# Attention scores in three fp32r products instead of one fp32 product

## The chip, the cores and the metric

The kernel runs on one core of one Trainium2 chip. The metric is the time of one execution on the device in microseconds, as the median of several runs. Engines are named as in the profile: PE (TensorE, matmuls), PEld (TensorE, loads of the stationary operand), DVE (VectorE), ACT (ScalarE), POOL (GpSimd), SP (SyncE, which only issues DMAs here).

## The reference

Attention with a local window and global tokens over 8 batches and 8 heads, and behind it a two-layer network on all tokens (4352 tokens, 512 to 2048 to 512, softplus between). All of it in float32:

```python
k_all = np.concatenate([k_g, k_l], axis=2); v_all = np.concatenate([v_g, v_l], axis=2)
out_g = np.matmul(sm(scale * np.matmul(q_g, k_all.transpose(0, 1, 3, 2))), v_all)
mask = np.abs(pos[:, None] - pos[None, :]) <= 32
s_ll = np.where(mask, scale * np.matmul(q_l, k_l.transpose(0, 1, 3, 2)), -1000000000.0)
s_lg = scale * np.matmul(q_l, k_g.transpose(0, 1, 3, 2))
out_l = np.matmul(sm(np.concatenate([s_lg, s_ll], axis=-1)), v_all)
attn = np.concatenate([out_g, out_l], axis=2)          # 8 x 8 x (32 + 512) x 64
x = attn.transpose(0, 2, 1, 3).reshape(8 * 544, 512)
h = x @ w_in
out = (np.maximum(h, 0) + np.log1p(np.exp(-np.abs(h)))) @ w_out
```

## The kernel before

Two heads lie side by side on the 128 partitions (64 dimensions each), so there are 32 pairs of heads, m = 0 to 31, four to a batch. The first M0 = 6 pairs are done in a form of their own, at the start, while the weights arrive. The pairs m = 6 to 31 go through the functions `load`, `scores`, `maxima`, `probs`, `totals`, `values` and `normalise`. Each has three pieces p = 0, 1, 2, each with its own slice of queries and keys.

`scores(m, p)` computes the scores of one piece for both heads: two parts, each 128 keys (the stationary operand) against 192 queries (96 in the second part of p = 2). Head 0 uses partitions 0 to 63, head 1 partitions 64 to 127, and they write different PSUM banks. So one piece is 2 parts x 2 heads = 4 matmuls in fp32. DVE then adds the mask (L325) and takes maxima (L326). In the pairs m = 6 and 7 (`m < MPE`) the mask is added by a matmul instead.

The network is done batch by batch in 16 tiles of 128 hidden units. Its float32 operands are split into two halves in fp32r, a high half (`xh`, `gh`, slice 0 of `wi` and `wo`) and a low half (`xl`, `gl`, slice 1), and each product is made of three: high x high, high x low, low x high. For a tile, `hpart` makes h (24 matmuls of 512 columns in two calls), `act` makes the softplus (three steps on ACT, one on DVE), its high half gh on ACT (L547) and its low half gl on POOL (L548), and `opart` adds gh and gl times `wo` to four output tiles o (24 matmuls in two calls). `opart` comes one or two tiles behind. The weights are turned into float32 and split in `abs_w`, `bits_w` and `halves_w` (L481 to L499) while batch 0 runs. At the start of a batch `split_x` makes xh and xl from the attention's output (L453, L454).

Each `pieces()` entry has a due number, and `moe_items` counts the network's progress on the same scale (48 per batch, 12 per pair). The main loop issues network items and, whenever a due number is reached, the next attention piece. So a score piece stands between two runs of network matmuls on PE, about every 9 us, and a `values` piece once per pair. The code is recorded in this order, and a scheduler then sets the order on each engine by a simulated timeline. All matmuls are chained in the order written (`mm`), so it does not move them among themselves. It moves work on DVE, ACT and POOL.

Buffers that matter here: `raw` (queries and keys as loaded, three), and the tag `x`, whose two buffers hold the exponentials of the first six pairs and are free after that.

Of the kernel before, what the change touches and what calls it, by code (L numbers as in the profile page):

```python
# [8 lines left out]
F32 = mybir.dt.float32  # L9
F32R = mybir.dt.float32r  # L10
# [3 lines left out]
ALU = mybir.AluOpType  # L14
# [5 lines left out]
P = 128  # L20
# [4 lines left out]
QW = (288, 288, 192)  # L25
KWID = (256, 256, 256)
# [3 lines left out]

M0 = 6
MPE = 8
VAL = 22
TOT = 18
STEP = 3
# [14 lines left out]
def windows(ap2d, start, stride, count, width):  # L50
    base = ap2d[:, start:start + width]
    return bass.AP(base.tensor, base.offset, [list(base.ap[0]), [stride, count], [1, width]])
# [3 lines left out]
def moe_over_global_local_attention(  # L56
# [11 lines left out]
    nc = tc.nc  # L68
    PSUM = bass.MemoryType.PSUM
    const = ctx.enter_context(tc.tile_pool(name="const", bufs=1))  # L70
    pl = ctx.enter_context(tc.tile_pool(name="pl", bufs=2))
# [20 lines left out]
    for o, w, base, sign in ((32, 32, 0, 1), (64, 32, -96, -1), (96, 128, 32, 1), (96, 128, 32, -1)):  # L92
        r = mask0[:, 0, 1, o:o + w]
# [26 lines left out]
    def after(i, what):  # L120

        if what in order:
            tc.add_manual_dep(i.ins, order[what].name, mybir.DependencyInfo(mybir.DependencyClass.NoSync, mybir.DependencyReason.DATA), reason="order")
        return i

    def mm(*a, **k):
        order["pe"] = after(nc.tensor.matmul(*a, **k), "pe").ins  # L127


    M = B * H // 2  # L130
    st = {}
# [153 lines left out]
    def load(m, p):  # L285
        w = QW[p] + KWID[p]
        raw = pl.tile([P, 544], F32, tag="raw", name=f"raw{m}_{p}", bufs=3)
        order["load"] = nc.sync.dma_start(out=raw[:, :w], in_=qk[m - M0, :, EW[p]:EW[p] + w]).ins
        st["raw", m, p] = raw

    def load_v(m):
        t = pl.tile([P, 2, 6, D], F32, tag="v", name=f"v{m}", bufs=2)
        nc.sync.dma_start(out=t.rearrange("p h c d -> p (h c d)"), in_=v[m - M0])
        st["v", m] = t

    def scores(m, p):
        raw = st.pop(("raw", m, p))
        q = QW[p]
        if "o" not in banks:
            ps = ps_s.tile([P, 2, 512], F32, tag=("oA", "oB")[(3 * m + p) % 2], name=f"s_ps{m}_{p}")  # L300
        else:
            ps = ps_a.tile([P, 2, 512], F32, tag="a", name=f"s_ps{m}_{p}")
        parts = ((0, 0, 192), (192, 96, 192 if p < 2 else 96))
        pe_mask = m < MPE
        masks = (mask[:, 0:192], mask[:, 192:384] if p < 2 else mask5)
        for i, (o, qs, w) in enumerate(parts):
            ks = q + 128 * i
            for h in range(2):
                r = slice(64 * h, 64 * h + 64)
                mm(ps[:, h, o:o + w], lhsT=raw[r, ks:ks + P], rhs=raw[r, qs:qs + w],  # L310
                   start=True, stop=not pe_mask, skip_group_check=True)
            for h in range(2 if pe_mask else 0):
                mm(ps[:, h, o:o + w], lhsT=ident, rhs=masks[i], start=False, stop=True, skip_group_check=True)
        if p == 0:
            st["mt", m] = pl.tile([P, 348], F32, tag="mt", name=f"mt{m}", bufs=2)
            nc.gpsimd.memset(windows(st["mt", m], 0, 36, 3, 3), LOW)
        mt = st["mt", m]
        nb = 12 if p < 2 else 9
        s = pl.tile([P, 2, 32 * nb], F32, tag="s" if p < 2 else "s2", name=f"s{m}_{p}", bufs=4 if p < 2 else 2)
        if pe_mask:  # L320
            nc.scalar.copy(s, ps[:, :, 0:32 * nb])  # L321
        else:
            for o, mk in ((0, mask[:, 0:384]),) if p < 2 else ((0, mask[:, 0:192]), (192, mask5)):
                w = mk.shape[1]
                nc.vector.tensor_tensor(s[:, :, o:o + w], ps[:, :, o:o + w], mk.unsqueeze(1).to_broadcast([P, 2, w]), op=ALU.add)  # L325
        order["scores"] = nc.vector.tensor_reduce(windows(mt, 3 + 12 * p, 36, 2, nb), s.rearrange("p h (b k) -> p h b k", k=32),  # L326
                                axis=AX.X, op=ALU.max, apply_transpose=True).ins
        st["s", m, p] = s
# [20 lines left out]
    def maxima(m):  # L349
        e = fold(st.pop(("mt", m)), ALU.max)  # L350
        for a in range(1, 4):
            i = nc.vector.tensor_copy(e[32 * a:32 * a + 32, 0:42], e[0:32, 0:42]).ins  # L352
        order["maxima"] = i
        st["e", m] = e

    def probs(m, p):
        s, e = st["s", m, p], st["e", m]
        k = QW[p] // 32
        mb = pl.tile([P, 2, 288], F32, tag="mb", name=f"mb{m}_{p}", bufs=2)
        nc.vector.transpose(mb[:, :, :QW[p]].rearrange("p h (s k) -> p h s k", k=32),  # L360
                            windows(e, 7 * p, 21, 2, k).unsqueeze(3).to_broadcast([P, 2, k, 32]))
        for h in range(2):
            if p < 2:
                sw = s[:, h].rearrange("p (c w) -> p c w", w=192)
                nc.gpsimd.tensor_tensor(sw, sw, windows(mb[:, h], 0, 96, 2, 192), op=ALU.subtract)  # L365
        if p == 2:
            nc.gpsimd.tensor_tensor(s[:, :, 0:192], s[:, :, 0:192], mb[:, :, 0:192], op=ALU.subtract)
            nc.gpsimd.tensor_tensor(s[:, :, 192:288], s[:, :, 192:288], mb[:, :, 96:192], op=ALU.subtract)
        nc.scalar.activation(s, s, AF.Exp, scale=0.125)  # L369
        if p == 0:  # L370
            st["zt", m] = pl.tile([P, 348], F32, tag="zt", name=f"zt{m}", bufs=2)
            nc.gpsimd.memset(windows(st["zt", m], 0, 36, 3, 3), 0.0)
        nb = 12 if p < 2 else 9
        nc.vector.tensor_reduce(windows(st["zt", m], 3 + 12 * p, 36, 2, nb), s.rearrange("p h (b k) -> p h b k", k=32),  # L374
                                axis=AX.X, op=ALU.add, apply_transpose=True)

    def totals(m):
        e = fold(st.pop(("zt", m)), ALU.add)
        nc.vector.tensor_scalar(e[0:32, 0:42], e[0:32, 0:42], 1e-9, None, op0=ALU.add)
        nc.vector.reciprocal(e[0:32, 0:42], e[0:32, 0:42])  # L380
        for a in (2, 3, 1):
            o = 21 * (a // 2)
            nc.vector.tensor_copy(e[32 * a:32 * a + 32, 0:21], e[0:32, o:o + 21])
        rb = st["rb", m] = pl.tile([P, 640], F32, tag="rb", name=f"rb{m}", bufs=1)
        nc.vector.transpose(rb.rearrange("p (s k) -> p s k", k=32), e[:, 0:20].unsqueeze(2).to_broadcast([P, 20, 32]))

    def values(m):

        vt = st["v", m]
        ps = st["vs", m] = ps_a.tile([P, 2, 512], F32, tag="a", name=f"v_ps{m}")  # L390
        flat = ps.rearrange("p a q -> p (a q)")
        for p in range(NPC):
            s = st.pop(("s", m, p))
            for i, (o, qs, w) in enumerate(((0, 0, 192), (192, 96, 192 if p < 2 else 96))):
                c = OUT[p] + qs
                for h in range(2):
                    mm(flat[64 * h:64 * h + 64, c:c + w], lhsT=vt[:, h, 2 * p + i], rhs=s[:, h, o:o + w],
                       start=p < 2 and i == 0, stop=True, skip_group_check=True)
# [17 lines left out]
    def pieces():  # L416
        def piece(*fs):
            def go():
                for f in fs:
                    f()  # L420
            return go
        ps = []
        for m in range(M0, M):
            for p in range(NPC):
                fs = [lambda m=m, p=p: scores(m, p)]
                if m + 1 < M:
                    fs.append(lambda m=m, p=p: load(m + 1, p))
                if p == 2:
                    fs.append(lambda m=m: maxima(m))
                    fs += [lambda m=m, q=q: probs(m, q) for q in range(NPC)]  # L430
                ps.append((12 * m + 4 * p, piece(*fs)))
            ps.append((12 * m + TOT, lambda m=m: totals(m)))
            fs = [lambda m=m: values(m), lambda m=m: normalise(m)]
            if m + 2 < M:
                fs.append(lambda m=m: load_v(m + 2))
            ps.append((12 * m + VAL, piece(*fs)))
        ps.sort(key=lambda t: t[0])
        return ps
# [173 lines left out]
    def loads(upto):  # L612
        while wk[0] < min(upto, len(order_w)):
            if order_w[wk[0]]:
                load_w(*order_w[wk[0]])
            wk[0] += 1
# [12 lines left out]
    for p in range(NPC):  # L629
        load(M0, p)  # L630
    load_v(M0)
    load_v(M0 + 1)
    loads(W_PRE + 1)
    first = 12 * (H // 2 - 1) + VAL + STEP
    pcs = pieces()
# [5 lines left out]
    n = len(steps)  # L641
# [6 lines left out]
    for k in range(-2, n + 2):  # L648
# [9 lines left out]
        if held:  # L658
            r = bits_w(*held)
# [91 lines left out]
```

## Time and profile before

| | |
|---|---|
| median of 3 runs | 1004.74 us (1004.15 to 1005.12) |
| the profiled execution: its time | 1005.01 us |
| the profiled execution: its span | 1003.2 us |
| PE busy | 966.0 us, 96% |
| DVE, ACT, POOL busy | 645.8, 517.5, 446.1 us |
| first and last score matmul of a loaded piece | 73.5 and 822.3 us |
| mean granted PE clock | 0.987 |

The time of an execution holds its span and a little around it (1.8 us here). In a group's row stand the line, engine and operation, output and inputs with their sizes, the count, busy time in us, mean duration in ns, and the idle time of the engine just before with what ended it. Matmuls overlap in their pipeline, so their durations add up to more than the time they occupy; the chain of work shows the time that each adds. "x8" in a timeline is eight instructions that follow each other. All matmuls but the bf16 masks are shown as "f32", fp32r ones too.

### The profile page before, as it was taken

Reading aid. Unit: us, or ns where it says so; the run is one execution under the profiler, and the core shown is the slowest. Engines: PE = TensorE matmul, PEld = TensorE weight load, DVE = VectorE, ACT = ScalarE, POOL = GpSimd, SP = SyncE. Lnnn points to the kernel's source line nnn. Section 1 sums busy time; section 2 is a strip of 40 time slices with the busy share of each in tenths; the row PEclk is TensorE's granted clock in tenths of the full one; section 3 lists DMA queues with packets and bytes.
Section 4 is the critical chain, followed back from the end, with each engine's and each line's share of the span. In section 5 each row is a group of like instructions: output and inputs, shape, how many; then the busy total and the mean of one; then the engine's idle time right before and its main releaser. Section 6 shows DMA issues by size and latency. Waiting matters only on the chain.

```text
span 1003.2 us, 14264 instructions
## 1 busy us (share of the span) xinstructions
PE 966.0 (96%) x5151; PEld 755.1 (75%) x5151; DVE 645.8 (64%) x1348; ACT 517.5 (52%) x918; POOL 446.1 (44%) x603
## 2 busy tenths in 40 slices
PE   6798989899999999999999999999999999999996
PEld 4576767677777777777777777777777778888895
DVE  6885979856678766776667677776677665211210
ACT  5787656544445544454454444554445445444452
POOL 5664776524444444453345444444435344222221
PEclk9999989989999999999999999999999999999998
DMA  9824322211112111121112111211112100100000
GB/s 354 310 74 144 112 83 60 58 63 48 40 49 90 49 37 48 49 85 43 47 34 90 40 49 49 70 58 49 48 39 89 47 2 16 50 1 1 22 22 21
DMA packets 34302, 66.19 MB, mean 66 GB/s; under 512 B 7608, under 2 KB 11448, under 8 KB 34232
## 3 DMA queue, kind: packets, MB, share of 16 engines
q1 hardware_dynamic: 33416, 65.19, 20.4%
q8 instruction: 40, 0.66, 0.3%
q14 instruction: 30, 0.25, 0.1%
q10 hardware_dynamic: 816, 0.10, 0.1%
HBM read 55.84 MB, written 9.44 MB: 65 GB/s over the span
## 4 chain that ended last, share of the span: by engine, by line
PE 79%; DVE 1%; POOL 0%; issue 0%; ACT 0%; DVEq 0%; POOLq 0%
PE o L127 35%; PE h L127 34%; PE s_ps L127 5%; PE v_ps L127 5%; DVE xl L454 1%; DVE zt L374 0%; POOL wo L499 0%; DVE mb L360 0%; POOL gl L548 0%; DVE wbitswo L490 0%; DVE e L544 0%; ACT ot L566 0%; DVE wlastwo L493 0%; DVE mt L352 0%; DVE mt L342 0%
## 5 line engine op out<-in xcount | busy, mean ns | idle before, releaser
L127 PE MATMUL o<-wo,gh 128*128 128x512 f32 x1088 | 347.5, 400 | 6.2 <-ACT gh L547 4.9
L127 PE MATMUL h<-xh,wi 128*128 128x512 f32 (+1 forms) x1152 | 351.1, 388 | 1.2 <-DVE e L544 0.7
L548 POOL TENSOR_TENSOR gl<-e,gh 128x512 fp32r<-128x512 f32 x136 | 177.8, 1307 | 333.2 <-ACT gh L547 271.1
L127 PEld LDWEIGHTS h<-xh,wi 128*128 128x128 f32 x1152 | 210.3, 190 | 51.4 <-issue 5.6
L127 PEld LDWEIGHTS o<-wo,gh 128*128 128x128 f32 x1088 | 200.9, 189 | 58.3 <-ACT gh L547 5.8
L544 DVE SCALAR_TENSOR_TENSOR e<-h,e 128x512 f32<-128x512 f32 x136 | 93.0, 684 | 234.4 <-ACT e L543 213.9
L127 PE MATMUL h<-xl,wi 128*128 128x512 f32 (+1 forms) x576 | 220.5, 383 | 0.0
L127 PE MATMUL o<-wo,gl 128*128 128x512 f32 x544 | 216.2, 397 | 2.5 <-POOL gl L548 2.5
L541 ACT ACTIVATE e<-h 128x512 f32<-128x512 f32 x136 | 81.3, 598 | 232.2 <-PE h L127 232.2
L547 ACT CAST gh<-e 128x512 fp32r<-128x512 f32 x136 | 84.3, 620 | 112.6 <-DVE e L544 112.6
L365 POOL TENSOR_TENSOR s<-s,mb 128x384 f32<-128x384 f32 x104 | 107.0, 1060 | 51.1 <-DVE mb L360 51.1
L127 PEld LDWEIGHTS h<-xl,wi 128*128 128x128 f32 x576 | 109.0, 189 | 22.7
L127 PEld LDWEIGHTS o<-wo,gl 128*128 128x128 f32 x544 | 102.9, 189 | 27.1 <-POOL gl L548 3.3
L543 ACT ACTIVATE e<-e,one 128x512 f32<-128x512 f32 x136 | 98.4, 723 | 4.2
L542 ACT ACTIVATE e<-e 128x512 f32<-128x512 f32 x136 | 85.7, 630 | 3.4
L325 DVE TENSOR_TENSOR s<-s_ps,mask 128x768 f32<-128x768 f32 (+1 forms) x96 | 64.7, 695 | 29.4 <-PE s_ps L127 29.4
L369 ACT ACTIVATE s<-s 128x768 f32<-128x768 f32 (+1 forms) x78 | 61.7, 790 | 37.1 <-POOL s L365 34.7
L374 DVE TRANSPOSE_TENSOR_REDUCE zt<-s 128x24 f32<-128x768 f32 (+1 forms) x78 | 69.9, 902 | 6.3 <-ACT s L369 4.7
L326 DVE TRANSPOSE_TENSOR_REDUCE mt<-s 128x24 f32<-128x768 f32 (+1 forms) x78 | 69.3, 888 | 5.8 <-ACT s L321 5.1
L127 PEld LDWEIGHTS s_ps<-raw 64*128 64x128 f32 x624 | 48.7, 186 | 29.6 <-issue 22.1
L127 PE MATMUL s_ps<-raw 64*128 64x192 f32 (+1 forms) x624 | 70.1, 340 | 0.7 <-ACT e_g L174 0.7
L127 PEld LDWEIGHTS v_ps<-s,v 128*64 128x64 f32 x624 | 42.5, 137 | 14.3 <-issue 9.0
(134 smaller groups left out, 881.9 us busy)
## 6 DMA issues: line engine op xcount, KB each, us to landing
raw<-in_qk SPq DMA_DIRECT2D x52, 272.0 KB, 2.7
v<-in_v SPq DMA_DIRECT2D x26, 384.0 KB, 3.1
out<-ot SPq DMA_DIRECT2D x34, 256.0 KB, 2.1
wiraw<-in_w_in SPq DMA_DIRECT2D x16, 512.0 KB, 9.1
woraw<-in_w_out SPq DMA_DIRECT2D x16, 512.0 KB, 8.6
raw<-in_qk SPq DMA_DIRECT2D x26, 224.0 KB, 2.5
v<-in_v SPq DMA_DIRECT2D x6, 512.0 KB, 6.0
raw<-in_qk SPq DMA_DIRECT2D x6, 416.0 KB, 7.8
```

Of the source, the lines that this page charges most:

```text
L127: order["pe"] = after(nc.tensor.matmul(*a, **k), "pe").ins
L325: nc.vector.tensor_tensor(s[:, :, o:o + w], ps[:, :, o:o + w], mk.unsqueeze(1).to_broadcast([P, 2, w]), op=ALU.add)
L326: order["scores"] = nc.vector.tensor_reduce(windows(mt, 3 + 12 * p, 36, 2, nb), s.rearrange("p h (b k) -> p h b k", k=32), axis=AX.X, op=A ...
L365: nc.gpsimd.tensor_tensor(sw, sw, windows(mb[:, h], 0, 96, 2, 192), op=ALU.subtract)
L369: nc.scalar.activation(s, s, AF.Exp, scale=0.125)
L374: nc.vector.tensor_reduce(windows(st["zt", m], 3 + 12 * p, 36, 2, nb), s.rearrange("p h (b k) -> p h b k", k=32), axis=AX.X, op=ALU.add, a ...
L541: nc.scalar.activation(e, ph, AF.Abs)
L542: nc.scalar.activation(e, e, AF.Exp, scale=-1.0)
L543: nc.scalar.activation(e, e, AF.Ln, bias=one)
L544: nc.vector.scalar_tensor_tensor(e, ph, 0.0, e, op0=ALU.max, op1=ALU.add)
L547: nc.scalar.copy(gh, e)
L548: nc.gpsimd.tensor_tensor(gl, e, gh.bitcast(F32), op=ALU.subtract)
```

## The change

Pairs from m = 9 on (`SPLIT`) get their queries and keys split like the network's operands. A new function `split_qk` reads a loaded `raw` tile and writes a tile with two halves: the high one by a cast to fp32r on ACT, the low one by a subtraction on POOL. `scores` then makes each product as high x high + high x low + low x high, 12 matmuls to a piece instead of 4. The split of a piece is issued right behind the scores of the piece before it. Its tile takes the two buffers of the tag `x`. The pairs below 9 are unchanged.

```diff
+SPLIT = 9
...
+    def split_qk(m, p):
+
+        raw, w = st.pop(("raw", m, p)), QW[p] + KWID[p]
+        t = st["halves", m, p] = pl.tile([P, 2, 544], F32R, tag="x", name=f"qk{m}_{p}", bufs=2)
+        nc.scalar.copy(t[:, 0, :w], raw[:, :w])
+        nc.gpsimd.tensor_tensor(t[:, 1, :w], raw[:, :w], t[:, 0, :w].bitcast(F32), op=ALU.subtract)
...
     def scores(m, p):
-        raw = st.pop(("raw", m, p))
...
+        if m >= SPLIT:
+            t = st.pop(("halves", m, p))
+            products = ((t[:, 0], t[:, 0]), (t[:, 0], t[:, 1]), (t[:, 1], t[:, 0]))
+        else:
+            raw = st.pop(("raw", m, p))
+            products = ((raw, raw),)
         for i, (o, qs, w) in enumerate(parts):
             ks = q + 128 * i
-            for h in range(2):
-                r = slice(64 * h, 64 * h + 64)
-                mm(ps[:, h, o:o + w], lhsT=raw[r, ks:ks + P], rhs=raw[r, qs:qs + w],
-                   start=True, stop=not pe_mask, skip_group_check=True)
+            for n, (kt, qt) in enumerate(products):
+                for h in range(2):
+                    r = slice(64 * h, 64 * h + 64)
+                    mm(ps[:, h, o:o + w], lhsT=kt[r, ks:ks + P], rhs=qt[r, qs:qs + w],
+                       start=n == 0, stop=n == len(products) - 1 and not pe_mask, skip_group_check=True)
...
                 fs = [lambda m=m, p=p: scores(m, p)]
+                then = (m, p + 1) if p < 2 else (m + 1, 0)
+                if SPLIT <= then[0] < M:
+                    fs.append(lambda then=then: split_qk(*then))
                 if m + 1 < M:
                     fs.append(lambda m=m, p=p: load(m + 1, p))
```

How it stands on the engines, at two places. First PE in batch 1, at the piece p = 2 of pair 11. `o1_3` is an output tile of batch 1, `h1_11` the hidden tile 11 of batch 1, `s_ps11_2` the piece's scores; the numbers at the end count tiles. Before:

```order
L127 MATMUL o1_3_2163<-wo8_1319,gh1_8_2534 128x512 x2
L127 MATMUL o1_3_2163<-wo8_1319,gl1_8_2535 128x512
L127 MATMUL s_ps11_2_2643<-raw11_2_2414 128x192 x2
L127 MATMUL s_ps11_2_2643<-raw11_2_2414 128x96 x2
L127 MATMUL h1_11_2685<-xh1_0_2016,wi10_1230 128x512 x2
```

and now:

```order
L128 MATMUL o1_3_2188<-wo8_1319,gh1_8_2614 128x512 x2
L128 MATMUL o1_3_2188<-wo8_1319,gl1_8_2615 128x512
L128 MATMUL s_ps11_2_2734<-qk11_2_2668 128x192 x6
L128 MATMUL s_ps11_2_2734<-qk11_2_2668 128x96 x6
L128 MATMUL h1_11_2787<-xh1_0_2030,wi10_1230 128x512 x2
```

Nothing moved on PE; the piece alone has three times as many matmuls, and so at all 69 pieces.

Second POOL at the end of batch 0. `s8_*` are the exponentials' inputs of pair 8, `zt8` its sums, `wo15` the last tile of weights, `gl0_15` the low half of the last hidden tile of batch 0. Before:

```order
L367 TENSOR_TENSOR s8_2_1862<-s8_2_1862,mb8_2_1893 128x2x192
L368 TENSOR_TENSOR s8_2_1862<-s8_2_1862,mb8_2_1893 128x2x96
L316 MEMSET mt10_2278 128x3x3
L339 COPY zt8_1884<-zt8_1884 32x75 x3
L499 TENSOR_TENSOR wo15_1920<-wlastwo_1918,wo15_1920 128x512
L548 TENSOR_TENSOR gl0_15_1977<-e0_15_1971,gh0_15_1976 128x512
```

and now:

```order
L381 TENSOR_TENSOR s8_2_1862<-s8_2_1862,mb8_2_1896 128x2x192
L382 TENSOR_TENSOR s8_2_1862<-s8_2_1862,mb8_2_1896 128x2x96
L330 MEMSET mt10_2322 128x3x3
L353 COPY zt8_1887<-zt8_1887 32x75 x3
L297 TENSOR_TENSOR qk9_2_2112<-raw9_2_1869,qk9_2_2112 128x448
L516 TENSOR_TENSOR wo15_1923<-wlastwo_1921,wo15_1923 128x512
L565 TENSOR_TENSOR gl0_15_1980<-e0_15_1974,gh0_15_1979 128x512
```

The subtraction of pair 9's piece 2 now stands behind the copies of zt8 and ahead of wo15 and gl0_15. Its cast stands likewise just ahead of wo15's cast on ACT.

## The prediction

> **What bounds the kernel now.** I read the page first: how busy each engine is, and the chain of work that ended last.
>
> ```profile
> span 1003.2 us, 14264 instructions
> PE 966.0 (96%) x5151; PEld 755.1 (75%) x5151; DVE 645.8 (64%) x1348; ACT 517.5 (52%) x918; POOL 446.1 (44%) x603
> PE 79%; DVE 1%; POOL 0%; issue 0%; ACT 0%; DVEq 0%; POOLq 0%
> PE o L127 35%; PE h L127 34%; PE s_ps L127 5%; PE v_ps L127 5%; DVE xl L454 1%; DVE zt L374 0%; POOL wo L499 0%; DVE mb L360 0%; POOL gl L548 0%; DVE wbitswo L490 0%; DVE e L544 0%; ACT ot L566 0%; DVE wlastwo L493 0%; DVE mt L352 0%; DVE mt L342 0%
> ```
>
> TensorE carries the chain, and the scores (s_ps) are only 5% of it, about 50 us. So the ceiling of any gain is small, and each score piece pays its change in full wherever TensorE has no gap. The second view cuts the span into stretches; I asked for one batch of the middle (430 to 540 us) and for the turn from batch 0 to batch 1.
>
> ```profile
> 200.00:210.00 10.00, 8.61 (x23) 6.39 (x24) 4.99 (x14) 1.67 (x4) 2.45 (x3) 0.66 0.14 52
> 430.31:539.77 109.46, 109.46 (x577) 84.91 (x577) 79.22 (x175) 53.54 (x86) 49.65 (x72) 1.00 0.19 54
> ```
>
> The columns are TensorE, its weight loads, VectorE, ScalarE, GpSimd, granted clock, DMA share, GB/s. In the middle TensorE has no gap at clock 1.00. At 200 us it has one, at a granted clock of 0.66.
>
> **What a score piece costs before.** The chain in order of time shows two pieces between runs of 12 fp32r matmuls (start, length, what):
>
> ```profile
> 453.99 2.79 PE h L127 x12
> 456.78 0.85 PE s_ps L127 x8
> 457.63 2.96 PE o L127 x12
> ...
> 466.19 0.72 PE s_ps L127 x8
> ```
>
> The timeline of the weight loads shows what happens in the first of them:
>
> ```profile
> 456.71 0.63 PEld L127 LDWEIGHTS s_ps<-raw 64*128 64x128 f32 x8 [0.36 <-DVE zt L379]
> 456.72 0.29 PEld L127 LDWEIGHTS s_ps<-raw 64*128 64x128 f32 x3
> 456.98 0.19 PEld L127 LDWEIGHTS s_ps<-raw 64*128 64x128 f32 x2
> 457.14 0.19 PEld L127 LDWEIGHTS s_ps<-raw 64*128 64x128 f32 x2
> 457.56 0.30 PEld L127 LDWEIGHTS o<-wo,gh 128*128 128x128 f32 x2 [0.23 <-ACT e L541]
> ```
>
> A piece writes 4 matmuls and the trace shows 8: each fp32 matmul runs as two passes. The loads come two by two (one per head, on the two halves of the rows), so there are 4 slots of a pair. Loads 2 to 4 (456.72, 0.29 long) end at 457.01; a load lasts 0.19, so the second pair begins at 456.82, 0.11 after the first. The third begins at 456.98 and the fourth at 457.14, each 0.162 later, which is 192 columns at two cycles and 2.4 GHz (0.160) plus 0.002. So a slot is set by its columns, and the load of the next slot runs under it. From first load to the load of the following o: 0.108 (first load) + 3 x 0.162 + 0.160 (last stream) + r = 0.85, so r = 0.096 for changing over. The 0.72 of the piece p = 2, whose last two slots have 96 columns (0.080), is then 0.108 + 2 x 0.162 + L + 0.080 + 0.096, which leaves L = 0.112 for a slot whose columns would take only 0.082. That slot is set by its weight load. Three other rows, of the timeline and of the groups, bear on this load:
>
> ```profile
> 64.77 0.74 PEld L127 LDWEIGHTS o0g<-p0g1gh,v 128*128 128x128 f32 x6 [0.28 <-issue]
> L127 PEld LDWEIGHTS h<-xh,wi 128*128 128x128 f32 x1152 | 210.3, 190 | 51.4 <-issue 5.6
> L127 PEld LDWEIGHTS s_ps<-raw 64*128 64x128 f32 x624 | 48.7, 186 | 29.6 <-issue 22.1
> ```
>
> From the chain, for the rate of fp32r:
>
> ```profile
> 974.47 2.79 PE o L127 x12
> 982.88 2.82 PE h L127 x24
> ```
>
> Six loads of 128 columns with only 64 columns to stream between them take 0.74, so (0.74 - 0.19) / 5 = 0.11 each: the floor again. The fp32r loads of wi last 190 ns, the fp32 loads of the scores 186, so I expect the same floor for both. In fp32r, 512 columns take 2.79 / 12 = 0.233 and 256 take 2.82 / 24 = 0.1175: 0.45 ns a column plus 0.002, or 0.089 for 192 columns and 0.046 for 96.
>
> **The change, part by part.** 23 pairs of heads (m = 9 to 31) change, 46 pieces with p < 2 and 23 with p = 2. Each has 6 slots of one fp32r pass where it had 4 slots of one fp32 pass.
>
> *Score pieces.* Streaming falls from 4 x 0.162 to 6 x 0.089, but no slot can be shorter than its load. That price, s, is not in the trace for fp32r with 64 rows. Its low end is 0.112 (same weights, in fp32), its high end 0.1175 (fp32r, 256 columns, which the columns alone explain). Both are near; I take 0.115.
> - p < 2: 0.108 + 5 x 0.115 + 0.087 + 0.096 = 0.866, against 0.85: +0.016, times 46 = +0.7 us (ends: 0 and +1.3).
> - p = 2: 0.108 + 5 x 0.115 + 0.044 + 0.096 = 0.823, against 0.72: +0.103, times 23 = +2.4 us (ends +2.0 and +2.7).
> Sum +3.1 us (+2.0 to +4.0). The two edges (first load, r) may differ for fp32r by some 0.02 either way, 1.4 us over 69 pieces; I take 0 and keep it for the range.
>
> The Trainium skill (TensorE: Matmul & The Clock Gate, What overlaps and what doesn't) says that a weight load overlaps running matmuls only where the row group differs. The trace differs: the third pair of loads begins at 456.98, as the second pair of matmuls starts on the same rows, and 0.162 has no room for 0.108 + 0.160 in turn. If that rule held for fp32r alone, the sum would be that of the third rival below.
>
> *The split: 69 casts on ScalarE, 69 subtractions on GpSimd.* Priced by the same kind of work on 512 columns:
>
> ```profile
> L547 ACT CAST gh<-e 128x512 fp32r<-128x512 f32 x136 | 84.3, 620 | 112.6 <-DVE e L544 112.6
> L548 POOL TENSOR_TENSOR gl<-e,gh 128x512 fp32r<-128x512 f32 x136 | 177.8, 1307 | 333.2 <-ACT gh L547 271.1
> ```
>
> and the timeline around the last gl of batch 1:
>
> ```profile
> 310.29 1.29 POOL L548 TENSOR_TENSOR gl<-e,gh 128x512 fp32r<-128x512 f32 x1 [3.99 <-issue]
> 314.74 0.39 PE L127 MATMUL o<-wo,gl 128*128 128x512 f32 x1
> ```
>
> A cast of 544 columns is 0.66 us, a subtraction 1.39 (448 columns: 0.54 and 1.14). A batch adds 8 and 4 of them: 7.4 us to ScalarE's 53.5 and 15.7 to GpSimd's 49.6, of 109.5. The halves are made a whole piece (some 9 us, 456.78 to 466.19) before they are read. What waits behind a subtraction on GpSimd is gl, which TensorE reads. The last gl of batch 1 ends at 311.58 and is first read at 314.74, a cover of 3.2 us against one subtraction of 1.39. So I cost it at nothing in batches 1 to 7; without cover it would be up to 1.39 a piece. The q/k load now waits for the subtraction in place of the scores, and comes earlier: nothing, at a DMA share of 0.19.
>
> *The turn from batch 0 to 1.* Here there is no cover. The rows of GpSimd, ScalarE and TensorE:
>
> ```profile
> 198.53 1.18 POOL L339 COPY zt<-zt 32x75 f32<-32x75 f32 x3 [3.04 <-DVE zt L374]
> 199.82 1.29 POOL L499 TENSOR_TENSOR wo<-wlastwo,wo 128x512 fp32r<-128x512 f32 x1
> 201.06 1.28 POOL L548 TENSOR_TENSOR gl<-e,gh 128x512 fp32r<-128x512 f32 x1
> 199.07 0.62 ACT L498 CAST wo<-wlastwo 128x512 fp32r<-128x512 f32 x1 [2.30 <-DVE wlastwo L493]
> 202.40 0.80 PE L127 MATMUL o<-wo,gl 128*128 128x512 f32 x1 [0.73 <-POOL gl L548]
> 202.99 1.05 PE L127 MATMUL o<-wo,gh 128*128 128x512 f32 x2
> 208.97 0.62 PE L127 MATMUL o<-wo,gh 128*128 128x512 f32 x2
> ```
>
> The subtraction of qk9_2 is put on GpSimd's queue between the copies of zt and wo, so wo and gl come 1.14 later and so does TensorE, which reads that gl at once (201.06 + 1.28 = 202.34). (The cast stands ahead of wo's on ScalarE, where 2.30 us are idle: nothing.) From 202.40 to about 208.5 a pair of matmuls takes 1.05 instead of 0.62, at half the clock. If full speed returns at the same moment, 1.14 fewer microseconds are spent at half speed and half of the delay is won back: +0.6 us (ends 0 and +1.14).
>
> **Sum.** +3.1 + 0.6 = +3.7 us. The profiled execution took 1005.01 us around its span of 1003.2, 0.27 above the median of 1004.74, so on the median the forecast is 1008.4 us. The difference is 0.4%; about 0.2% (2.0 us) is what a measurement here can tell from no change.
>
> **Rivals.**
> 1. *Streaming decides, faster.* If the fp32r load of 64 rows took less than 0.089, each slot would be 0.089: p < 2 is 0.736 (-0.114), p = 2 is 0.607 (-0.113), 69 pieces -7.8, with the turn -7.2: 997.5 us. Its point is a load step of 0.104: there the pieces give back what the turn costs. For it: fp32 needs two passes where fp32r needs one. Against it: L = 0.112 for these very weights, and loads of 186 and 190 ns. The Trainium skill (FP8 and Floating Point Precision, TensorE Precision Notes) counts four passes for true fp32, so three products would be three quarters of the work; 0.160 for half a matmul of 192 columns agrees with four, but the rule counts no loads.
> 2. *fp32r is slower below 256 columns.* No fp32r matmul of the trace is narrower, so the 0.45 ns a column is not shown at 192. At the fp32 pass's two cycles a slot is 0.162: p < 2 is 1.17 (+0.32), p = 2 is 0.99 (+0.27), sum +21, with the turn about 1027. At four cycles a slot is 0.322 (p < 2 +1.28, p = 2 +0.93): +81, about 1086. For it: only the missing row. Against it: 256 and 512 columns lie on one line.
> 3. *Loads or heads in turn.* If a load could not run under the stream of its own rows, a slot is 0.112 + 0.089: p < 2 +0.45, p = 2 +0.45, sum +31, 1036 us. If the two heads did not run side by side, 12 slots of 0.112 give +0.67 and +0.76, sum +48, 1054. Against both: fp32 does neither here.
>
> **How the numbers follow.** Forecast (slots at the load step) 0.80; rival 1: 0.05; rival 2: 0.10; rival 3: 0.05. Range: the forecast's own bounds, 1004.74 + 2.0 + 0 - 1.4 = 1005.3 and 1004.74 + 4.0 + 1.1 + 1.4 = 1011.2, opened to 1005 and 1012 for small waits in batch 0, where GpSimd also gets two subtractions. What it leaves out is the 0.20 of the rivals. Faster: rival 1, 0.05. The same: the part of the forecast up to 1006.75 (low step, no delay at the turn), 0.17. Slower: the rest, 0.63 + 0.10 + 0.05 = 0.78.
>
> **What would show it.** In the profile after, a score piece should be 12 matmuls in 0.85 to 0.88 for p < 2 and 0.81 to 0.84 for p = 2, its loads in pairs 0.112 to 0.118 apart; TensorE still without a gap from 210 to 850 us; gl and wo about 1.1 us later near 201. It is wrong if pairs lie 0.09 apart (rival 1), 0.16 or more (rival 2), if loads come singly (rival 3), or if TensorE waits for gl or qk in the middle.

## The result, and the profile after

The changed kernel takes 1009.96 us (median of 4 runs, 1009.79 to 1011.17) against 1004.44 us (4 runs, 1003.79 to 1005.12) for the kernel before, measured beside it: ratio 1.0057, 95% interval 1.004 to 1.0075. That is 5.5 us slower. The forecast was 1008.4 us, 3.7 us slower.

The head of the page after the change, the same lines as the prediction shows of before: span, busy time of each engine, and the chain by engine.

```profile
span 1007.7 us, 15027 instructions
PE 968.8 (96%) x5427; PEld 763.0 (76%) x5427; DVE 660.5 (66%) x1348; ACT 553.0 (55%) x987; POOL 534.5 (53%) x672
PE 79%; POOL 1%; issue 1%; ACT 0%; POOLq 0%
```

PE is busy 2.8 us more (968.8 against 966.0), and the span is 4.5 us longer, so part of the loss is idle time on PE. POOL has 88.4 us more to do. The stretches show where PE idles (PE, PEld, DVE, ACT, POOL, granted clock, DMA share, GB/s):

```profile
150.00:175.00 25.00, 24.23 (x120) 18.48 (x116) 23.79 (x39) 14.03 (x24) 18.17 (x18) 1.00 0.30 81
200.00:210.00 10.00, 5.88 (x13) 3.98 (x14) 8.00 (x18) 1.80 (x3) 4.79 (x7) 0.66 0.18 60
210.00:850.00 640.00, 640.00 (x3620) 503.71 (x3619) 463.63 (x994) 346.01 (x565) 371.55 (x478) 1.00 0.18 50
```

From 210 to 850 us PE has no gap, as forecast. At the turn to batch 1 it is busy 5.88 of 10 us, before 8.61. The first row is a place that the prediction did not look at: late in batch 0, where DVE is busy 23.79 of 25 us. Before the change PE had no gap there:

```profile
150.00:175.00 25.00, 25.00 (x120) 19.70 (x117) 23.13 (x40) 15.89 (x27) 17.32 (x18) 1.00 0.21 61
```

The chain of the changed kernel in order of time, in batch 3, shows the score pieces (p < 2, then p = 2):

```profile
456.91 2.79 PE h L128 x12
459.71 0.84 PE s_ps L128 x12
460.55 2.96 PE o L128 x12
...
469.10 0.80 PE s_ps L128 x12
```

and the timeline of the weight loads shows the first of them:

```profile
459.64 0.74 PEld L128 LDWEIGHTS s_ps<-qk 64*128 64x128 f32 x12 [0.36 <-issue]
```

Twelve loads, two by two, take 0.74. A load lasts 0.19, so the pairs lie (0.74 - 0.19) / 5 = 0.11 apart. The piece p < 2 went from 0.85 to 0.84, the piece p = 2 from 0.72 to 0.80.

By stage, the traces compare like this. Each time is that of the first matmul of h with xl in that batch or hidden tile (us; the two middle columns are experiments 1 and 2, told below):

| | before | no pair 9 | pair 9 with one subtraction | after |
|---|---|---|---|---|
| batch 0, hidden tile 0 | 87.16 | 87.48 | 87.47 | 87.54 |
| batch 0, hidden tile 15 | 185.8 | 186.1 | 186.2 | 188.2 |
| batch 1 | 205.12 | 205.50 | 206.53 | 208.44 |
| batch 2 | 316.14 | 316.79 | 317.17 | 318.67 |
| batch 6 | 754.01 | 755.93 | 756.32 | 757.81 |
| end | 1003.2 | 1005.7 | 1005.8 | 1007.7 |

Batches 2 to 5 take 109.47 us each before and 109.79 after: +0.32, which is 4 pieces p = 2 at +0.08. (The 0.01 that each of the eight pieces p < 2 is shorter does not show in a batch.) Most of the rest arises ahead of batch 1: +2.4 by tile 15, of which 0.4 is there at tile 0 already, ahead of the first split, then +0.9 at the turn, and 0.8 less in batch 1, some of it won back at half clock. A last 0.5 lies behind the last matmul, where both kernels do the same work.

Where the +2.4 comes from shows in the timelines of the stretch at 163 us. VectorE before, and after:

```profile
163.40 0.41 DVE L488 TENSOR_SCALAR wbitswo<-wbitswo 128x512 int32<-128x512 int32 x1
163.73 0.67 DVE L544 SCALAR_TENSOR_TENSOR e<-h,e 128x512 f32<-128x512 f32 x1
164.33 0.15 DVE L346 COPY zt<-zt 32x6 f32<-32x6 f32 x1
164.40 0.67 DVE L490 SCALAR_TENSOR_TENSOR wbitswo<-woraw,wbitswo 128x512 int32<-128x512 int32 x1
165.01 1.28 DVE L379 TENSOR_SCALAR zt<-zt 32x42 f32<-32x42 f32 x1
...
168.37 1.52 DVE L383 COPY zt<-zt 32x21 f32<-32x21 f32 x3
...
171.87 0.68 DVE L544 SCALAR_TENSOR_TENSOR e<-h,e 128x512 f32<-128x512 f32 x1
```

```profile
163.97 1.60 DVE L505 TENSOR_SCALAR wbitswo<-wbitswo 128x512 int32<-128x512 int32 x1
165.50 1.26 DVE L360 COPY zt<-zt 32x6 f32<-32x6 f32 x1
166.68 0.67 DVE L561 SCALAR_TENSOR_TENSOR e<-h,e 128x512 f32<-128x512 f32 x1
...
167.88 0.17 DVE L393 TENSOR_SCALAR zt<-zt 32x42 f32<-32x42 f32 x1
...
170.13 2.70 DVE L397 COPY zt<-zt 32x21 f32<-32x21 f32 x3
...
174.80 0.68 DVE L561 SCALAR_TENSOR_TENSOR e<-h,e 128x512 f32<-128x512 f32 x1
```

POOL after, in the same stretch, with the two subtractions that the change puts into batch 0 (qk9_0 and qk9_1):

```profile
162.96 2.33 POOL L297 TENSOR_TENSOR qk<-raw,qk 128x544 fp32r<-128x544 f32 x1
165.24 1.49 POOL L516 TENSOR_TENSOR wo<-woraw,wo 128x512 fp32r<-128x512 f32 x1
...
169.78 1.57 POOL L297 TENSOR_TENSOR qk<-raw,qk 128x544 fp32r<-128x544 f32 x1
171.29 1.32 POOL L516 TENSOR_TENSOR wo<-woraw,wo 128x512 fp32r<-128x512 f32 x1
```

VectorE's shift of weight bits (L505, a TENSOR_SCALAR) grows from 0.41 to 1.60, a copy of zt (L360) from 0.15 to 1.26, and three copies (L397) from 1.52 to 2.70. The first two end close to the end of the POOL subtraction beside them: the shift at 165.57 (that of qk9_0 ends at 165.29), the copy at 166.76 (that of wo ends at 166.73). The copy of 32 x 6 elements also stands ahead of e now. Between 163.4 and 171.9 VectorE does the same work in both kernels, and the delay of the second e follows from the rows: 0.57 that VectorE was late already, + 1.19 (shift) + 1.11 (copy) + 1.18 (three copies) - 1.11 (the TENSOR_SCALAR of zt, 1.28 before and 0.17 now) = 2.94, against 174.80 - 171.87 = 2.93. The matmul of h that needs the buffer this e frees is late, as PE's timeline shows:

```profile
175.53 0.74 PE L128 MATMUL h<-xh,wi 128*128 128x512 f32 x2 [1.23 <-DVE e L561]
```

The turn goes as forecast, later by these delays. The chain there:

```profile
202.06 1.15 POOL qk L297
203.21 1.22 POOL wo L516
204.43 1.24 POOL gl L565
205.67 0.04 issue
205.71 2.08 PE o L128 x4
```

### The profile page after: what moved, and what is told of

Same layout as the page of the kernel before. It is cut to its first block, busy times and chain, and to the rows that moved or that the text cites. A ratio compares the mean times of both kernels' runs of the same rounds, so it can differ in the third digit from the quotient of the medians.

```text
span 1007.7 us, 15027 instructions
## 1 busy us (share of the span) xinstructions
PE 968.8 (96%) x5427; PEld 763.0 (76%) x5427; DVE 660.5 (66%) x1348; ACT 553.0 (55%) x987; POOL 534.5 (53%) x672
## 4 chain that ended last, share of the span: by engine, by line
PE 79%; POOL 1%; issue 1%; ACT 0%; POOLq 0%
PE o L128 34%; PE h L128 34%; PE s_ps L128 6%; PE v_ps L128 5%; POOL s L379 0%; POOL gl L565 0%; POOL s L381 0%; POOL wo L516 0%; POOL qk L297 0%; POOL zt L353 0%; POOL s L382 0%; ACT ot L583 0%; POOL mt L353 0%; POOL mt L330 0%; POOLq L297 0%
## 5 line engine op out<-in xcount | busy, mean ns | idle before, releaser
L379 POOL TENSOR_TENSOR s<-s,mb 128x384 f32<-128x384 f32 x104 | 106.6, 1058 | 6.6 <-DVE mb L374 6.6
L297 POOL TENSOR_TENSOR qk<-raw,qk 128x544 fp32r<-128x544 f32 (+1 forms) x69 | 91.3, 1322 | 30.4 <-ACT qk L296 25.5
L128 PEld LDWEIGHTS s_ps<-qk 64*128 64x128 f32 x828 | 51.3, 187 | 25.0 <-issue 23.1
L374 DVE STREAM_TRANSPOSE mb<-mt 128x576 f32<-128x576 f32 (+1 forms) x78 | 52.1, 693 | 23.4 <-POOL s L379 23.2
```

The lines of the kernel that those rows point to most:

```text
L297: nc.gpsimd.tensor_tensor(t[:, 1, :w], raw[:, :w], t[:, 0, :w].bitcast(F32), op=ALU.subtract)
```

## The experiments

Three terms stood to be told apart: the score pieces on PE, the splits in the middle of the run, and pair 9, whose three splits lie in batch 0 and at the turn. My theory was that the loss is the pieces p = 2, whose slots their weight loads set, and pair 9, whose subtractions on POOL come where PE has no cover; the rivals were splits that cost something in every batch, and slots that their columns set. All experiments are edits of the changed kernel, and all but two begin with `SPLIT = 10`, which leaves pair 9 in fp32 and so leaves out what happens ahead of batch 1. Times stand against the kernel before on the same chip.

**1. Without pair 9.**

```diff
-SPLIT = 9
+SPLIT = 10
```

> The change from pair 10 on, so that no split falls into batch 0. Theory A: the change costs 0.09 us in each piece p = 2 on TensorE (its slots last as long as their weight load), 22 x 0.09 = 2.0 us, and the rest of the loss came from three subtractions on GpSimd in batch 0, two of which slow VectorE down (about 2 us at 163 to 174 us) and one of which delays the last weights and gl. Then this gives 1004.4 + 2.0 = 1006.4 us, and batch 1 starts as before (205.1 us). Rival B: batch 0 has no part in it and all score pieces and splits lose a little everywhere: 22/23 of the loss, 1009.7 us.

Measured: 1007.57 us, ratio 1.0024 (1.0014 to 1.0033), so +2.4 us. Batch 1 starts 2.9 us earlier than with pair 9. About half of the loss is pair 9, which is one of 23 pairs.

**2. Pair 9 without its two subtractions in batch 0.** The low halves of its pieces 0 and 1 are only a cast on ACT (values other than the reference's, the same work on PE).

```diff
-        nc.gpsimd.tensor_tensor(t[:, 1, :w], raw[:, :w], t[:, 0, :w].bitcast(F32), op=ALU.subtract)
+        if m == SPLIT and p < 2:
+            nc.scalar.copy(t[:, 1, :w], raw[:, :w])
+        else:
+            nc.gpsimd.tensor_tensor(t[:, 1, :w], raw[:, :w], t[:, 0, :w].bitcast(F32), op=ALU.subtract)
```

> The changed kernel, but the low halves of pieces 0 and 1 of pair 9 are a second cast on ScalarE instead of a subtraction on GpSimd (their low half is then not the right one). Theory A: GpSimd's subtraction is what slows VectorE at 163 to 174 us; without it VectorE's single-input operations there are short again (0.4 and 0.15 us instead of 1.6 and 1.3) and TensorE reaches hidden tile 13 as before (173.7 instead of 176.1 us). The delay of the last gl stays. 1004.4 + 2.0 + 0.5 = 1006.9 us, with 1 us to either side. Rival C: ScalarE's casts or the later loads on SyncE's queue make the delay; both stay (ScalarE gets 1.2 us more), so 1009.5 to 1011 us.

Measured: 1007.4 us, ratio 1.0024 (1.0014 to 1.0033), the same as without pair 9. VectorE's timeline at the same place:

```profile
164.32 0.41 DVE L508 TENSOR_SCALAR wbitswo<-wbitswo 128x512 int32<-128x512 int32 x1
164.65 0.15 DVE L363 COPY zt<-zt 32x6 f32<-32x6 f32 x1
164.72 0.67 DVE L564 SCALAR_TENSOR_TENSOR e<-h,e 128x512 f32<-128x512 f32 x1
```

The copy still stands ahead of e, and ACT has even two casts more, but both short operations have their old length (POOL is idle there, from 163.35 to 165.16), and tile 15 starts at 186.2 instead of 188.2. So it is the subtraction on POOL that makes them long, not the order on VectorE and not ACT. The third subtraction, at the turn, is still there: batch 1 starts 1.03 us later than without pair 9, batch 2 0.38 us later, and in the medians nothing is left to see.

**3. Only the two subtractions of batch 0.** Pair 9 stays in fp32, but the halves of its pieces 0 and 1 are made and not used.

```diff
-SPLIT = 9
+SPLIT = 10
...
-        raw, w = st.pop(("raw", m, p)), QW[p] + KWID[p]
+        raw, w = st["raw", m, p] if m < SPLIT else st.pop(("raw", m, p)), QW[p] + KWID[p]
...
-                if SPLIT <= then[0] < M:
+                if SPLIT <= then[0] < M or then in ((9, 0), (9, 1)):
```

> from10 with the splits of pieces 0 and 1 of pair 9 put back into batch 0 and not used (pair 9's scores stay fp32). On GpSimd the first stands where the changed kernel has it, the second three places later; the split of piece 2 is left away. Theory A: the first subtraction meets VectorE's shift of weight bits and its copy of zt7 again, these last 1.6 and 1.3 us instead of 0.4 and 0.15, and hidden tile 13 comes at 175 to 176 us instead of 174.0; 1 to 2.5 us over from10. Rival F: it was the order or the scores of pair 9, not the subtraction; as from10, 1007.4 us.

Measured: 1012.26 us, ratio 1.007 (1.0057 to 1.0083). The shift and the copy are long again:

```profile
164.21 1.59 DVE L505 TENSOR_SCALAR wbitswo<-wbitswo 128x512 int32<-128x512 int32 x1
165.73 1.27 DVE L360 COPY zt<-zt 32x6 f32<-32x6 f32 x1
```

Tile 15 starts at 189.1 and batch 1 at 209.02, so the two subtractions alone bring back the whole delay ahead of batch 1, and more (208.44 in the changed kernel). The total went past what I expected. From batch 3 on a batch takes 110.37 us instead of 109.79: the scheduler set another order, and at each batch's end a copy of zt on VectorE is long beside the subtraction of a later split (POOL, 655.57 to 656.95) and holds up an e that PE needs. So the hold-up of batch 0 can come in the middle too, where the order lets it. The chain there:

```profile
655.91 1.06 DVE zt L360
656.97 0.60 DVE e L561
657.57 0.04 issue
657.62 3.03 PE h L128 x12
```

So the total of this run sizes nothing; its first 209 us do.

**4. The changed kernel again**, on the chip of experiments 6, 9 and 10, to see how firm its time is.

> The changed kernel once more, beside the next three on one chip, so that its distance to from10 and no_pool9_01 (both +2.4 us) can be read. Theory A: +2.0 for the pieces, about +2 for the two subtractions in batch 0 that slow VectorE, about +0.5 for the last gl: +4.5 us. Rival D: the first comparison's +5.5 is the true size and something of 1 us more is missing from the account.

Measured: 1010.95 us, ratio 1.0057 (1.0043 to 1.0071), the same ratio, which is +5.7, where my theory added up to +4.5. The interval still holds 4.5, but the rival, that about 1 us is missing from the account, is as well borne out. In its trace 0.8 us is lost by hidden tile 0 (87.98 against 87.16), ahead of the first split; tile 15 starts at 188.6, batch 1 at 208.91 and batch 2 at 319.82. Its stretch at half clock began at 204.5 instead of 202.5, and batch 1 took 110.9 us, against 110.2 in the first trace and 111.3 without pair 9: less of the delay was won back.

**5. The splits without the products.** Halves are made for all pieces from pair 10 and not used; the scores stay in fp32.

```diff
-        raw, w = st.pop(("raw", m, p)), QW[p] + KWID[p]
+        raw, w = st["raw", m, p], QW[p] + KWID[p]
...
-            t = st.pop(("halves", m, p))
-            products = ((t[:, 0], t[:, 0]), (t[:, 0], t[:, 1]), (t[:, 1], t[:, 0]))
+            st.pop(("halves", m, p))
+            raw = st.pop(("raw", m, p))
+            products = ((raw, raw),)
```

> As from10, but the scores stay fp32 products of the loaded queries and keys; the halves are made and not used. Theory A: the 66 casts and 66 subtractions of the middle are covered, so 1004.4 us, no change against before. Rival B: ScalarE's and GpSimd's added work delays what TensorE waits for, in every batch: 1006 to 1008 us.

Measured: 1011.52 us, ratio 1.006 (1.0047 to 1.0074), more than my theory (no change) and its rival (1006 to 1008) allowed. The waits of PE from 200 to 860 us and the chain at the end of batch 1 name the cause (what waits for what, us in total, times, the longest; then start, us, what):

```profile
PE o L128 <- POOL gl L566: 5.7, 6, 1.0
```

```profile
312.25 3.00 POOL s L380 x3
315.25 1.56 POOL gl L566
316.81 0.04 issue
316.85 1.20 PE o L128 x4
```

The last gl of the batch now stands on POOL behind four additions to s of 1 us each, and PE waits for it. In the changed kernel that gl stands ahead of them (from 206 to 860 PE waits 0.4 us in all, at the turn). The four additions, not the splits, are on the path here, put there by the order that the scheduler found for this variant.

**6. The same with the order restored.** My reading was that without products that read it nothing held a cast back, so that the scheduler issued it early and got another order; here each cast is tied behind the scores two pieces earlier.

```diff
-        nc.scalar.copy(t[:, 0, :w], raw[:, :w])
+        order["old"], order["mid"] = order.get("mid", order["pe"]), order["pe"]
+        after(nc.scalar.copy(t[:, 0, :w], raw[:, :w]), "old")
```

> split_only10 again (fp32 scores, halves made and not used from pair 10 on), but each cast is put behind the scores two pieces earlier, as it is in the changed kernel, so that gl of the last hidden tile stands ahead of the four subtractions of s on GpSimd's queue at each end of a batch and not behind them. Theory A: the splits of the middle are covered and split_only10's +6.4 us came from that order alone; this is within 0.6 us of before. Rival B: the splits' work itself costs in the middle; +3 to +6 us stay.

Measured: 1005.36 us, ratio 1.0005 (0.9996 to 1.0013). gl is ahead of the additions again, PE has no wait from 206 to 860 us, and batches 2 and 3 take 109.47 us each, as before the change. So the 66 casts and subtractions of pairs 10 to 31 cost nothing measurable in that order.

**7. The products without the splits.** One pair of halves is made and read by all pieces, so the scores of the other pieces are left out.

```diff
-        raw, w = st.pop(("raw", m, p)), QW[p] + KWID[p]
-        t = st["halves", m, p] = pl.tile([P, 2, 544], F32R, tag="x", name=f"qk{m}_{p}", bufs=2)
+        raw, w = st["raw", m, p], QW[p] + KWID[p]
+        t = st["halves"] = pl.tile([P, 2, 544], F32R, tag="x", name=f"qk{m}_{p}", bufs=2)
...
-            t = st.pop(("halves", m, p))
+            st.pop(("raw", m, p))
+            t = st["halves"]
...
-                if SPLIT <= then[0] < M:
+                if then == (SPLIT, 0):
```

> As from10, but all pieces from pair 10 on read the halves of piece 0 of pair 10, so there are three fp32r products and no splits but one (the scores of the other pieces are left out). Theory A: the pieces p = 2 alone carry it, 1006.4 us, as from10 within 0.5 us, with a piece of 0.84 (p < 2) and 0.80 us (p = 2) in the chain. Rival B: what from10 loses comes from the splits, so this is 1004.4 us.

Measured: 1007.28 us, ratio 1.0019 (1.0011 to 1.0028), as much as experiment 1 within the intervals. So the loss from batch 1 on is in the matmuls.

**8. The piece p = 2 in fp32, the pieces p < 2 in three products.**

```diff
-        if m >= SPLIT:
+        if m >= SPLIT and p < 2:
...
-                if SPLIT <= then[0] < M:
+                if SPLIT <= then[0] < M and then[1] < 2:
```

> from10 with the pieces p = 2 left in fp32; only p < 2 (192 columns in both parts) use three fp32r products. Theory A: p < 2 costs the same in both forms (0.84 against 0.85 us) and p = 2 carried from10's loss, so this is before within 0.6 us, 1005.0 us. Rival G: something else that all pieces from pair 10 share costs the 2 us; two thirds stay, 1006.5 us.

Measured: 1004.64 us, ratio 0.9996 (0.9986 to 1.0005). Three products on 192 columns cost what one fp32 product costs; the loss of experiment 1 is the 22 pieces p = 2, whose 96 columns a slot leave the load as the limit. That is 22 x 0.08 = 1.8 us of the 2.4 measured (1.4 to 3.3). In the trace of experiment 1 the rest is 0.3 us by tile 0 and 0.3 behind the last matmul, where the kernels do not differ.

**9. Two products.** The product of the low keys and the high queries is left out.

```diff
-            products = ((t[:, 0], t[:, 0]), (t[:, 0], t[:, 1]), (t[:, 1], t[:, 0]))
+            products = ((t[:, 0], t[:, 0]), (t[:, 0], t[:, 1]))
```

> from10 without the third product (low keys x high queries is left out), so 4 slots instead of 6. Theory A (a slot lasts as long as its weight load, 0.112): a piece is 0.63 (p < 2) and 0.58 us (p = 2), 0.22 less than from10 in both; 66 x 0.22 = 14.8 us less, 12 to 13 us faster than before. Rival E (the columns decide, 0.089 and 0.046): a piece loses 0.18 and 0.09, 10 us less than from10, 7.5 us faster than before.

Measured: 992.09 us, ratio 0.9868 (0.9854 to 0.9881). The chain:

```profile
452.96 0.62 PE s_ps L128 x8
...
462.09 0.58 PE s_ps L128 x7
```

Two slots fewer take 0.22 off each piece, 0.11 a slot, at 192 columns and at 96: 44 x (0.85 - 0.62) + 22 x (0.72 - 0.58) = 13.2 us, against 1005.03 - 992.09 = 12.9. It is the fastest of all kernels here, with less computed.

**10. Wider slots.** The slots of the pieces p < 2 stream 256 columns instead of 192 (one execution).

```diff
         for i, (o, qs, w) in enumerate(parts):
+            w = 256 if m >= SPLIT and p < 2 else w
```

> from10 with 256 moving columns instead of 192 in the pieces p < 2; the extra columns are overwritten or not read. Theory A: six slots of max(0.112, 0.1175) and a last stream that is 0.03 longer: 0.84 becomes 0.89 us, 44 pieces, +2.5 us over from10. Rival E (the columns decide): six slots longer by 0.029, 0.84 becomes 1.01, +7.5 us over from10.

Measured: 1008.39 us, and a piece of 0.91 in the chain:

```profile
457.13 0.91 PE s_ps L128 x12
```

That is the sum for slots at the 0.1175 that 256 columns take: 0.108 + 5 x 0.1175 + 0.1175 + 0.096 = 0.909 (0.89 was expected, worked out from slots of 0.112). Batches 2 to 5 take 110.25 us against 109.79 in experiment 1, so 0.06 a piece. The total is only 0.8 us above experiment 1, where 2.5 were expected: in this one execution the stretch at half clock at the turn lasted 3.41 us and not 6.83, and batch 1 took 110.4 us, against 111.3. So the piece carries the reading, and the total does not. From 96 to 192 columns a slot stays at 0.11, and at 256 it follows the columns. What 192 columns take by themselves is not seen, only that it is no more than 0.11.

## Why the prediction was right or wrong, point by point

**The sum.** +3.7 us was forecast, +5.5 measured (4.0 to 7.5 by the interval). The direction is right, and the time lies inside the range, above its middle. Two of the terms were off in opposite directions: the score pieces were forecast too large, and batch 0 was held at nothing. By their measured sizes the two terms that the sum did cost give 1.8 + 0.4 = 2.2 us, so that +3.7 came as near to +5.5 as it did is in part luck.

**Score pieces: mechanism right, size too large.** A slot takes the same 0.11 at 192 and at 96 columns (experiments 9 and 10), and that is the step of its weight loads. The term that was mis-sized is s: I took 0.115, between fp32's 0.112 and the 0.1175 of 256 columns, and the loads lie 0.11 apart. With the prediction's own sum that gives 0.108 + 5 x 0.11 + 0.087 + 0.096 = 0.841 and 0.798, which are the pieces measured, 0.84 and 0.80. So the piece p < 2 costs nothing (experiment 8; +0.7 forecast) and the pieces p = 2 23 x 0.08 = +1.8 us (+2.4 forecast). Together +1.8 where I had +3.1, a little under the low end of 2.0. The row nearest in kind, the same 64-row weights, was a better guide than the middle. The signs that the prediction gave (0.85 to 0.88, 0.81 to 0.84, loads 0.112 to 0.118 apart) are each missed by 0.01 or less, for the same reason.

One rival is not in the prediction: a fixed cost of a slot, whatever it loads. The rows of `values` speak against it. Its weights have 64 columns in place of 128, and its first two pairs of loads in the same stretch begin 0.06 apart:

```profile
472.82 0.14 PEld L128 LDWEIGHTS v_ps<-s,v 128*64 128x64 f32 x2 [0.36 <-issue]
472.88 0.14 PEld L128 LDWEIGHTS v_ps<-s,v 128*64 128x64 f32 x2
```

Its last two slots, of 96 columns in fp32, begin 0.08 apart (474.50 and 474.58), where the same columns behind weights of 128 columns took 0.112 before. So the step goes with the size of the load.

**Splits in batches 1 to 7: right.** PE has no gap from 210 to 850 us, and experiment 6 finds no cost. That hangs on the order, though: with gl behind four additions (experiment 5), or with a copy of zt beside a split's subtraction and an e behind it (experiment 3), PE waits at the ends of the batches. The cover of 3.2 us that I read from one gl holds for the place where that gl stands.

**The turn: right.** qk9_2 at 202.06, wo and gl behind it. Its 1.15 us of subtraction delay batch 1 by 1.03, and 0.38 are left at batch 2 (experiments 1 and 2), where I had 1.14 and +0.6. That half clock gives part of the delay back is seen there, but it depends on when that stretch falls (experiment 4) and how long it lasts (experiment 10).

**Batch 0: the step that failed.** The prediction knew of the two subtractions there and left them to the range as "small waits", because it asked only what stands behind a subtraction in POOL's queue ("What waits behind a subtraction on GpSimd is gl"). It did not ask which other engine's work grows while POOL subtracts. They hold up VectorE, which was 93% busy there before the change (23.13 of 25 us). Against experiment 2 they delay tile 15 by 2.0 us and batch 1 by 1.9, and in the medians experiment 2 gives 1.0024 where the changed kernel has 1.0057: 0.0033, some 3.3 us, on intervals that would also bear 2 or 5. So about 2 to 3.5 us of the 5.5 are this term, as much as the score pieces or more. How much it is beyond the 1.9 of the trace stays open.

The trace of before already held this to be read. A TENSOR_SCALAR on 42 elements takes 1.28 us in the rows of VectorE above (L379, 165.01 to 166.29) beside this row of POOL, and 0.17 after the change, where POOL was idle:

```profile
164.24 2.01 POOL L499 TENSOR_TENSOR wo<-woraw,wo 128x512 fp32r<-128x512 f32 x1 [1.82 <-ACT wo L498]
```

The subtraction ends at 166.25, and the TENSOR_SCALAR with it.

**The rivals.** Streaming (rival 1) has slots of 0.089, and needed 0.104 or less to be faster at all; 0.11 decides against it, by little. fp32r slow below 256 columns (rival 2) and loads or heads in turn (rival 3) are out: 12 matmuls take 0.84 on 192 columns and 0.91 on 256.

## What to carry to other kernels

Count what a piece costs by its slots, and take for each slot the longer of its weight load and its columns: here three products on 192 columns cost as much as one in fp32, on 96 columns they cost more, and taking a product away pays 0.11 us a slot at either width. When an engine gets more work, price not only what queues behind it but also which operations of the other engines grow while it runs, and look first where such an engine has little idle time (93% busy here) and TensorE needs its work soon after. When an experiment changes what a scheduler sees, compare the orders on the engines, here at the ends of the batches, before you compare the totals.

## What the runs showed of the hardware

VectorE and POOL hold each other up, in both directions. Beside a POOL subtraction, VectorE's TENSOR_SCALAR and COPY do not end until about the end of the subtraction (0.41 to 1.60, 0.15 to 1.26, and in the trace of before 1.28 against 0.17), down to a copy of 32 x 6 elements. Not every operation on one tensor does so: a RECIPROCAL takes 0.40 both beside a subtraction (166.81 before) and with POOL idle (202.61 before).

Operations on two tensors go both ways. At 164.40 before the change VectorE's operation on woraw and wbitswo keeps its 0.67, and it is POOL's subtraction of wo that takes 2.01, against 1.29 at the turn. In batch 1 after the change POOL's subtraction of qk keeps its 1.39, and it is VectorE's subtraction of xl that takes 1.21, against 0.33 with no subtraction beside it:

```profile
306.51 1.39 POOL L297 TENSOR_TENSOR qk<-raw,qk 128x544 fp32r<-128x544 f32 x1
306.83 1.21 DVE L471 TENSOR_TENSOR xl<-xa,xh 128x128 fp32r<-128x128 f32 x1
...
308.44 0.33 DVE L471 TENSOR_TENSOR xl<-xa,xh 128x128 fp32r<-128x128 f32 x1
```

The Trainium skill (GPSIMD Engine Reference, Specifications) says that GpSimd shares its access to SBUF with VectorE, and that they contend where a VectorE instruction runs in a 2-port mode or has two inputs in SBUF. The traces agree for the two inputs (1.21 against 0.33); which mode the TENSOR_SCALAR and COPY run in no run here shows. Which of the two engines pays is not settled by the kind of operation, and what settles it stays open.

A stretch at half clock lasted 6.83 us at the turn in the traces of before, after and the repeat, and 3.41 us in experiment 10. Its start moved from trace to trace (201.7 before, 202.5 after, 204.5 in the repeat), not with PE's gap alone: from the changed kernel to its repeat the gap begins 0.5 us later (199.4 and 199.9) and the stretch 2.0.
